# Moving the second batch's first stage, turn and low-rank step and the next pair's preparation forward in the loop of a fused Fourier and mixer kernel, and the batch's DRAM writes to the sync queue

## The chip, the cores and the metric

The kernel runs on one core of a Trainium2 chip. The metric is the device time of one execution, in microseconds (us). Executions are compared in the fast state only: a run that took over 1.5% longer than the fastest of its kernel counts as slow and is left out of the ratios. Ratios are the mean time of one kernel's fast runs over the mean of the other's fast runs of the same rounds, so they are not quite the ratios of the medians quoted beside them, which are over all runs (one slow of nine in run 3, two of six in run 7, two of 22 in run 9, one of six in run 10).

In the lines of the profile PE is TensorE, DVE is VectorE, ACT is ScalarE and POOL is GpSimd (called Pool here); SPq and ACTq are the issues of DMA transfers by the sync engine and by ScalarE. L260 is line 260 of the kernel, `teps<-g,us` means that tile teps is written from g and us, and x25 that the line stands for 25 instructions.

## The reference, cut to what matters

```python
X = np.fft.fft(np.fft.fft(x, axis=1), axis=2).real      # x: 8 batches, 3136 positions, 256 channels
h = X.transpose(0, 2, 1) @ U @ V                        # low rank (32) over the positions
u = X + h.transpose(0, 2, 1)
out = u + np.maximum(u @ w_ch1, 0.0) @ w_ch2            # 256 -> 1024 -> 256 channels
```

## The kernel before

The 8 batches go in four pairs. For each pair a loop of 13 chunks does the two channel products (`mlp1`, `mlp2`); each chunk has four steps, so a pair has 52 loop steps. Between the products, the loop also carries work for the batches to come. This other work is hung on step numbers. In the traces TensorE runs its matmuls in the order of the program, so a piece that is not ready holds up all that follows: when g was not there for the low-rank step, TensorE stood idle for 6.22 us with loop steps still to do.

The way of one batch: x is loaded, stage one (`s1`) makes z with matmuls, z is written to DRAM (`zturn`) and read back in another order as g (the **turn**), the **low-rank step** makes te from g (or, for later pairs, from z) and spreads it over the lower half of g, and stage three (`s3`) makes q, the input of the products. The **receipt** is here the time from the end of the issue of a batch's last DRAM write to the issue of its turn, where nothing else stands between the two: for the first batch 2.9 us (about 21.1 to 24.00). In pair 0 the first batch is done before the loop, but for nine of its thirteen s3 groups, which stand in steps 1 to 8. The second batch's s1, turn, low-rank step and s3 stand in the loop, as does the preparation of pair 1.

```python
def s1_single(pr, b, tiles, evacs, engines):
    ...
        evacs[n](z[:, 2 * s:2 * s + 2, :], ps[:])              # ScalarE and VectorE in turn
        if n % 2:                                              # two DRAM writes after every second step
            for i in range(2):
                engines(n)[i].dma_start(out=dst, in_=z[64 * i:64 * i + 64, ...])

def turn(pr, b, parts, engines=(nc.sync,)):                    # g <- zturn, on the sync queue
    ...
        engines[i % len(engines)].dma_start(out=g[0:64, k0:k1], in_=src[:, k0:k1, :])

def te_single(pr, b, spread):                                  # the low-rank step: 25 matmuls of 64x64 weights
    ps = psd.tile([P, 2, D], FP32, tag="ps", name="teps")
    for k in range(NK1):
        nc.tensor.matmul(ps[0:64, 0, :], us[:, k], pr.g[b][0:64, k, :], start=(k == 0), stop=(k == NK1 - 1))
    te_out(pr, b, ps, slice(0, 64), spread)                    # VectorE, then the spread on Pool

def mlp2(ch, t):
    ...
    nc.scalar.copy(om[:, 0:n], ch.po[:, 0:n, 1])               # in odd steps: ScalarE, VectorE twice,
    nc.vector.tensor_tensor(ob[:, 0:n, 0:P], ch.po[:, 0:n, 0], om[:, 0:n], op=AL.add)
    nc.vector.tensor_tensor(ob[:, 0:n, P:D], ch.po[:, 0:n, 0], om[:, 0:n], op=AL.subtract)
    ...                                                        # and four outputs on the sync queue

def place_next(nx, a, gap, s3lo):                              # the next pair
    for c, (load, fn, fd) in enumerate(load_steps(nx)):        # 8 chunks: load, fold on Pool, fold on VectorE, two s1
        for o, f in [(0, load), (4, fn), (7, fd), (9, s1[2 * c]), (10, s1[2 * c + 1])]:
            at[int(a + gap * c) + o].append(f)
    e = int(a + gap * 7) + 11
    place([lambda: (turn(nx, 0, whole), turn(nx, 1, whole))], e, e + 1)
    place(te_steps(nx, spread_pool), e, e + 3)
    place(s3_steps(nx, 0, copy_dve), s3lo, NS)
```

The PSUM tiles of s1, s3 and the low-rank step share one pool (`psd`) of two buffers.

Of the kernel before, what the change touches and what calls it, by code (L numbers as in the profile page):

```python
# [22 lines left out]
def kernel(  # L23
# [9 lines left out]
    nc = tc.nc  # L33
# [115 lines left out]
    def load_steps(pr):  # L149

        for c in range(8):
            def load(c=c):
                pr.chunks.append(load_pair_chunk(pr.p, c))
            yield load, (lambda c=c: fold_pair_chunk(pr.chunks[c])), (lambda c=c: fold_pair_chunk_d(pr.chunks[c]))
# [31 lines left out]
    def s1_single(pr, b, tiles, evacs, engines):  # L186


        if pr.z is None:
            pr.z = zpool.tile([P, 32, D], BF16, tag="z", name="z")  # L190
        z = pr.z[:, 16 * b:16 * b + 16]
        zdb = zd[pr.p % 2, b]

        def step(n, s):
            xs, l = tiles[s // 2], 4 * (s % 2)
            ps = psd.tile([P, 2, D], FP32, tag="ps", name="ps")
            todo = []
            for i in range(2):
                o = ps[64 * i:64 * i + 64]
                if s == 0 and i == 0:  # L200
                    todo.append([(o[:, 1], xs[:, 1], 0), (o[:, 0], xs[:, 0], 1), (o[:, 0], x32[b][:], 2)])
                else:
                    todo.append([(o, xs[:, l + 2 * i:l + 2 * i + 2], 0)])
            prods = []
            for parts in todo:
                pp = []
                for o, y, t in parts:
                    fe, fo, fn = (Fs[:, 3 * t + i].rearrange("p k c -> p (k c)") for i in range(3))
                    pp += [(o[..., 0:129], fe, y[..., 0:129]), (o[..., 1:128], fe, y[..., 255:128:-1]),
                           (o[..., 129:256], fo, y[..., 1:128]), (o[..., 129:256], fn, y[..., 255:128:-1])]  # L210
                prods.append(pp)
            for m in range(max(len(p) for p in prods)):
                for pp in prods:
                    if m < len(pp):
                        o, f, y = pp[m]
                        nc.tensor.matmul(o, f, y, start=(m == 0), stop=True, skip_group_check=True)  # L216
            evacs[n](z[:, 2 * s:2 * s + 2, :], ps[:])
            if n % 2:
                q = s // 2
                for i in range(2):  # L220
                    dst = bass.AP(zd.tensor, zdb.offset + (8 * q + 2 * i) * D, [[32 * D, 64], [4 * D, 2], [1, 2 * D]])
                    engines(n)[i].dma_start(out=dst, in_=z[64 * i:64 * i + 64, 4 * q:4 * q + 4].rearrange(
                        "p (i h) d -> p i (h d)", h=2))

        for n, s in enumerate([2, 3, 4, 5, 6, 7, 1, 0]):
            yield lambda n=n, s=s: step(n, s)

    def turn(pr, b, parts, engines=(nc.sync,)):
        g = gpool.tile([P, NK1, D], BF16, tag=f"g{b}", name="g")
        src = zd[pr.p % 2, b].rearrange("k cn d -> cn k d")  # L230
        for i, (k0, k1) in enumerate(parts):
            engines[i % len(engines)].dma_start(out=g[0:64, k0:k1], in_=src[:, k0:k1, :])
        pr.g[b] = g

    def te_out(pr, b, ps, hb, spread):
        te = ypool.tile([P, D], BF16, tag="te", name="te")
        nc.vector.tensor_tensor(te[64:128, :], ps[hb, 0, :], mask[hb, :], op=AL.mult)  # L237
        spread(pr.g[b], te)
# [17 lines left out]
    def te_single(pr, b, spread):  # L256
# [4 lines that stand above are left out]
        te_out(pr, b, ps, slice(0, 64), spread)  # L261

    def spread(parts):
        def run(g, te):
            src = te[64:128].bitcast(I32)
            for eng, k0, k1 in parts:
                eng.tensor_copy(g[64:128, k0:k1].bitcast(I32), src.unsqueeze(1).to_broadcast([64, k1 - k0, D // 2]))  # L267
        return run

    def two(row, a, b, n):  # L270

        v = row[:, a:a + n]
        return bass.AP(row.tensor, v.offset, [list(v.ap[0]), [b - a, 2], [1, n]])

    def s3_steps(pr, b, evac):

        if pr.q is None:
            pr.q = qpool[pr.p % 2].tile([P, 2, 6272], BF16, tag="q", name="q")

        def mm(o, k1, blk, st):  # L280
            lt = pr.g[b][:, k1, blk::2]
            r = T[:, k1, 0:64] if k1 == 0 else T[:, k1, :].rearrange("p (s j) -> p s j", s=2)
            nc.tensor.matmul(o, lt, r, start=st, stop=True, skip_group_check=True)  # L283

        def step(g, blk):
            ps = psd.tile([P, 2, 256], FP32, tag="ps", name="ps")
            k0 = 4 * g
            for u in range(4):
                us = slice(u * 64, (u + 1) * 64)
                mm(ps[:, 0, us] if k0 + u == 0 else ps[:, :, us], k0 + u, blk, u == 0)  # L290
            pl = b * 1600 + k0 * 64
            mi = 3200 + b * 1536 + (k0 - 1) * 64
            if g == 0:
                evac(pr.q[:, blk, pl:pl + 256], ps[:, 0, :])
                evac(pr.q[:, blk, mi + 64:mi + 256], ps[:, 1, 64:256])
            else:
                evac(two(pr.q[:, blk, :], pl, mi, 256), ps[:])

        def last():
            ps = psd.tile([P, 2, 2, 64], FP32, tag="ps", name="ps")  # L300
            k1 = NK1 - 1
            for blk in range(2):
                mm(ps[:, blk], k1, blk, blk == 0)
            for blk in range(2):
                evac(two(pr.q[:, blk, :], b * 1600 + k1 * 64, 3200 + b * 1536 + (k1 - 1) * 64, 64), ps[:, blk])

        for g in range(6):
            for blk in range(2):
                yield lambda g=g, blk=blk: step(g, blk)
        yield last  # L310
# [100 lines left out]
    part = [[None] * 4, [None] * 4]  # L411
# [208 lines left out]
    pairs = [first] + [Pair(p) for p in range(1, NP)]  # L620
# [3 lines left out]
    whole = [(0, NK1)]  # L624
    spread_pool = spread([(nc.gpsimd, 0, 9), (nc.gpsimd, 9, 17), (nc.gpsimd, 17, NK1)])

    def w2_fold(i):
        nc.vector.tensor_tensor(W2[:, :, i * P:(i + 1) * P], w2_f[:, :, 0], w2_f[:, :, 1],  # L628
                                op=(AL.subtract if i else AL.add))
# [39 lines left out]
    def plan(p):  # L669

        at = [[] for _ in range(NS)]

        def place(steps, lo, hi):
            steps = list(steps)
            for i, s in enumerate(steps):
                at[lo + i * (hi - lo) // len(steps)].append(s)

        def place_next(nx, a, gap, s3lo):

            s1 = list(s1_steps(nx, copy_act))  # L680
            for c, (load, fn, fd) in enumerate(load_steps(nx)):
# [7 lines that stand above are left out]
        cur = pairs[p]  # L689
        if p == 0:  # L690
            rest = []
            place(s3b0[4:8], 1, 3)
            place(s3b0[8:], 4, 9)
            place([lambda: w2_fold(0), lambda: w2_fold(1)], 2, 4)
            place([late_tables], 5, 6)
            place([load_uz], 12, 13)
            place([lambda: rest.append(pair_tables())], 6, 7)
            place([lambda: rest[0]()], 10, 11)
            place(s1_single(cur, 1, part[1], [copy_act, copy_dve] * 4, lambda n: (nc.scalar, nc.scalar)), 5, 13)
            place([lambda: turn(cur, 1, whole)], 13, 14)  # L700
            place([lambda: te_single(cur, 1, spread_pool)], 18, 19)
            place(s3_steps(cur, 1, copy_dve), 20, 32)
            place_next(pairs[1], 12, 2.5, 43)
        else:
            place(s3_steps(cur, 1, copy_dve), 3, 18)
            if p + 1 < NP:
                place_next(pairs[p + 1], 0, 3.4, 40)
        return at

    for i in range(len(chunks) + 1):  # L710
        cur = chunks[i] if i < len(chunks) else None
# [45 lines left out]
```

## Time and profile before

| | before |
|---|---|
| median | 491.05 us (489.51 to 491.84, 3 runs) |
| span of the profiled execution | 487.4 us |
| TensorE busy | 451.9 us |
| first wait: the low-rank step for g | 6.22 us, at 81.5 us |
| second wait: pair 1's s3 for g | 4.51 us, at 146.4 us |
| TensorE at half clock in the loop, up to pair 1 | 55.9 to 59.3, 86.6 to 96.8 and 151.4 to 154.8 us |

The lines themselves stand in the prediction below. The loop starts at 35.65 us with step 0. Step 2, which starts at 39.36 us, is used as a zero mark further down, as all that lies before it is the same code in all kernels here.

### The profile page before, as it was taken

How to read it: one execution, taken by the hardware profiler on the slowest of the kernel's cores; microseconds unless marked ns; L12 is line 12 of the kernel's file. 1: busy time of each engine (PE TensorE's matmuls, PEld its weight loads, DVE VectorE, ACT ScalarE, POOL GpSimd, SP SyncE). 2: the span in 40 equal slices, each digit the busy share in tenths (PEclk: the TensorE clock that was granted, in tenths of full speed). 3: DMA queues.
4: the chain of work that ended last, by engine and by line, in shares of the span. 5: the costliest groups of instructions: out<-in, count | busy, mean ns of one | idle time of the engine just before them, and what ended most of it. 6: DMA issues, size and time to landing. Idle time of an engine off the chain costs nothing.

```text
span 487.4 us, 9451 instructions
## 1 busy us (share of the span) xinstructions
PE 451.9 (93%) x3685; PEld 317.9 (65%) x3685; DVE 223.6 (46%) x512; ACT 286.1 (59%) x387; POOL 138.2 (28%) x143
## 2 busy tenths in 40 slices
PE   6878896899996999999999999999999999999992
PEld 2545564567774776766786776676777777767672
DVE  8954431086632537646425447647144344211211
ACT  6436355167752566677746556777655655666660
POOL 8442302295406025336042026534050000000000
PEclk9889899599998999999999999999999999999998
DMA  9978448568659245766386265576492222223322
GB/s 155 220 168 121 116 117 176 149 181 241 218 139 183 66 103 159 226 199 208 107 151 183 66 173 142 169 246 184 125 167 67 66 67 66 66 71 75 82 60 72
DMA packets 69297, 67.63 MB, mean 139 GB/s; under 512 B 17396, under 2 KB 62268, under 8 KB 69220
## 3 DMA queue, kind: packets, MB, share of 16 engines
q1 hardware_dynamic: 54100, 46.38, 38.3%
q0 software_dynamic: 11168, 12.92, 11.6%
q10 hardware_dynamic: 3984, 7.73, 4.7%
q8 instruction: 29, 0.48, 0.4%
q14 instruction: 16, 0.13, 0.1%
HBM read 35.95 MB, written 34.28 MB: 144 GB/s over the span
## 4 chain that ended last, share of the span: by engine, by line
PE 72%; DVE 10%; DMA 8%; SPq 3%; ACT 3%; issue 2%; ACTq 0%; POOL 0%; DVEq 0%; POOLq 0%
PE hps L334 29%; PE ops L345 28%; PE ps L283 4%; PE ops L348 4%; DMA g<-zturn 3%; DMA out_dram<-ob 3%; SPq L360 2%; PE ps L172 2%; ACT hT L336 2%; DVE q L79 2%; PE teps L260 2%; DMA xs<-in_x_dram 2%; PE teps L248 1%; DVE yb L122 1%; DVE ob L356 1%
## 5 line engine op out<-in xcount | busy, mean ns | idle before, releaser
L336 ACT ACTIVATE hT<-hps 128x1024 bf16<-128x1024 f32 (+1 forms) x208 | 202.8, 976 | 151.2 <-PE hps L334 142.0
L345 PE MATMUL ops<-W_91,hT 128*128 128x256 bf16 x1568 | 227.3, 275 | 1.1 <-DVE W_91 L628 1.1
L345 PEld LDWEIGHTS <-hT 128*128 128x128 bf16 x1568 | 146.3, 99 | 35.6 <-issue 0.8
L355 DVE TENSOR_TENSOR ob<-ops,om 128x256 f32<-128x256 f32 (+1 forms) x100 | 41.9, 419 | 195.0 <-ACT om L354 191.5
L334 PE MATMUL hps<-q,W1p 128*128 128x512 bf16 (+1 forms) x448 | 107.0, 362 | 2.4 <-DVE q L79 1.8
L334 PE MATMUL hps<-q,W1m 128*128 128x512 bf16 x384 | 100.0, 384 | 0.2 <-ACT hT L336 0.2
L131 POOL TENSOR_TENSOR y<-xa,xb 98x1020 f32<-98x1020 f32 (+1 forms) x24 | 54.8, 2282 | 126.2 <-DMA xa<-in_x_dram 123.0
L79 DVE CAST q<-ps 128x512 bf16<-128x512 f32 (+3 forms) x120 | 64.5, 559 | 32.4 <-PE ps L283 27.4
L334 PEld LDWEIGHTS <-W1p 128*128 128x128 bf16 x448 | 41.0, 98 | 30.2 <-issue 6.2
L348 PEld LDWEIGHTS <-q 128*128 128x128 bf16 x392 | 38.7, 99 | 22.6 <-issue 2.2
L334 PEld LDWEIGHTS <-W1m 128*128 128x128 bf16 x384 | 35.8, 99 | 26.4 <-issue 2.3
L283 PE MATMUL ps<-T,g 128*128 128x128 bf16 (+1 forms) x400 | 37.5, 219 | 7.2 <-DMA g<-zturn 4.5
L354 ACT COPY om<-ops 128x256 f32<-128x256 f32 (+1 forms) x100 | 36.8, 368 | 9.2 <-PE ops L345 8.3
L76 ACT CAST z<-ps 128x512 bf16<-128x512 f32 x57 | 33.5, 588 | 13.1 <-PE ps L172 10.9
L356 DVE TENSOR_TENSOR ob<-ops,om 128x256 f32<-128x256 f32 (+1 forms) x100 | 40.9, 409 | 0.0
L267 POOL COPY g<-te 64x1024 int32<-64x1024 int32 (+1 forms) x21 | 21.6, 1075 | 61.0 <-DVE te L237 61.0
L348 PE MATMUL ops<-Bp,q 128*128 128x128 f16 x200 | 38.6, 220 | 0.0
L283 PEld LDWEIGHTS <-g 128*128 128x128 bf16 x400 | 29.6, 98 | 13.1 <-POOL g L267 5.0
L348 PE MATMUL ops<-Bm,q 128*128 128x128 f16 x192 | 37.4, 221 | 0.0
L102 POOL DMA_INDIRECT xb<-in_x_dram,idx x24 | 25.4, 1059 | 10.9 <-PE ps L216 6.0
L122 DVE TENSOR_TENSOR yb<-y 98x508 bf16<-98x508 f32 (+1 forms) x24 | 27.2, 1134 | 0.8 <-POOL y L131 0.8
L172 PE MATMUL ps<-yb,F 98*128 98x258 bf16 (+1 forms) x108 | 18.9, 265 | 2.6 <-DVE q L79 2.4
(129 smaller groups left out, 220.3 us busy)
## 6 DMA issues: line engine op xcount, KB each, us to landing
out_dram<-ob SPq DMA_DIRECT2D x392, 64.0 KB
xa<-in_x_dram SPq DMA_DIRECT2D x24, 392.0 KB
g<-zturn SPq DMA_DIRECT2D x7, 800.0 KB
zturn<-z ACTq DMA_DIRECT2D x9, 512.0 KB
xs<-in_x_dram POOLq DMA_DIRECT2D x16, 196.0 KB, 8.6
w_f<-in_moe_w_ch_dram SPq DMA_DIRECT2D x2, 1024.0 KB
zturn<-z ACTq DMA_DIRECT2D x3, 448.0 KB
zturn<-z ACTq DMA_DIRECT2D x9, 128.0 KB
```

Source lines behind the costliest of these rows:

```text
L76: nc.scalar.copy(o, i)
L79: nc.vector.tensor_copy(o, i)
L122: nc.vector.tensor_tensor(o[:, :, 1:128], i[:, :, 1:128], i[:, :, 255:128:-1], op=AL.add)
L131: nc.gpsimd.tensor_tensor(ck.y[:, 0:n, 1:256], ck.xa[:, 0:n, 1:256], rb[:, :, 255:0:-1], op=AL.add)
L283: nc.tensor.matmul(o, lt, r, start=st, stop=True, skip_group_check=True)
L334: nc.tensor.matmul(ps[:, i, 0:n], (W1p if ch.sg > 0 else W1m)[:, blk, j], q[:, blk, c0:c0 + n], start=(blk == 0), stop=(blk == 1))
L336: nc.scalar.activation(ch.h[:, 2 * jp:2 * jp + 2, 0:n], ps[:, :, 0:n], AF.Relu)
L345: nc.tensor.matmul(ps, ch.h[:, j, t * P:(t + 1) * P], W2[:, j, :], start=(j == 0 and t % 2 == 0), stop=(j == JT - 1), skip_group_check=True)
L348: nc.tensor.matmul(ps[:, j], q[:, j, tk], (Bp if ch.sg > 0 else Bm)[:, j], start=False, stop=False, skip_group_check=True)
L354: nc.scalar.copy(om[:, 0:n], ch.po[:, 0:n, 1])
L355: nc.vector.tensor_tensor(ob[:, 0:n, 0:P], ch.po[:, 0:n, 0], om[:, 0:n], op=AL.add)
L356: nc.vector.tensor_tensor(ob[:, 0:n, P:D], ch.po[:, 0:n, 0], om[:, 0:n], op=AL.subtract)
```

## The change

The intent: do the second batch's stage one three steps sooner, so that its turn is back when TensorE comes to the low-rank step; keep ScalarE free of DMA issues; and start the next pair's loads four steps sooner, so that its turn too is back in time. Two things of no urgency are put off: the late tables (W1m and others) and the two loads of UZ, the table for the low-rank step of the later pairs. The whole change:

```diff
-            place([late_tables], 5, 6)
-            place([load_uz], 12, 13)
+            place([late_tables], 8, 9)
+            place([load_uz], 24, 25)
 ...
-            place(s1_single(cur, 1, part[1], [copy_act, copy_dve] * 4, lambda n: (nc.scalar, nc.scalar)), 5, 13)
-            place([lambda: turn(cur, 1, whole)], 13, 14)
-            place([lambda: te_single(cur, 1, spread_pool)], 18, 19)
-            place(s3_steps(cur, 1, copy_dve), 20, 32)
-            place_next(pairs[1], 12, 2.5, 43)
+            place(s1_single(cur, 1, part[1], [copy_act, copy_dve] * 4, lambda n: (nc.sync, nc.sync)), 2, 10)
+            place([lambda: turn(cur, 1, whole)], 10, 11)
+            place([lambda: te_single(cur, 1, spread_pool)], 15, 16)
+            place(s3_steps(cur, 1, copy_dve), 17, 29)
+            place_next(pairs[1], 8, 2.6, 44)
```

## The prediction

> **What bounds the kernel now.** I read the page first, then who waited for whom on TensorE, the timeline of TensorE and of the sync queue, the clock by the microsecond, and the chain of waits around the first loop steps.
>
> ```profile
> PE 451.9 (93%) x3685; PEld 317.9 (65%) x3685; DVE 223.6 (46%) x512; ACT 286.1 (59%) x387; POOL 138.2 (28%) x143
> PE   6878896899996999999999999999999999999992
> PEclk9889899599998999999999999999999999999998
> ```
> TensorE is the bound: 451.9 of 487.4 us busy. In the 40 slices of 12.2 us the poor ones are few: slice 8 (85 to 97 us) at clock 0.5, slice 13 (146 to 158 us) at busy 0.6.
>
> ```profile
> PE teps L260 <- DMA g<-zturn: 6.2, 1, 6.2
> PE ps L283 <- DMA g<-zturn: 4.5, 1, 4.5
> PE hps L334 <- DVE q L79: 1.8, 1, 1.8
> ```
> Columns: total us, times, longest. These three are all before 155 us; after 160 us TensorE waits 3.1 us in all. So only the start and the hand-over to pair 1 can give time.
>
> ```profile
> 29.15 2.91 PE L260 MATMUL teps<-g,us 64*64 64x256 bf16 x25
> ...
> 87.69 5.49 PE L260 MATMUL teps<-g,us 64*64 64x256 bf16 x25 [6.22 <-DMA g<-zturn]
> 93.11 1.89 PE L334 MATMUL hps<-q,W1m 128*128 128x512 bf16 x4
> ...
> 96.72 1.08 PE L334 MATMUL hps<-q,W1m 128*128 128x512 bf16 x4
> ```
> The same 25 low-rank matmuls take 2.91 us warm and 5.49 us after the wait. The step after them takes 96.72 - 93.11 = 3.61 us where a plain step takes 1.85 (73.92 to 75.77). The wait thus costs 6.22 + 2.58 + 1.76 = 10.6 us.
>
> ```profile
> 86.00:87.00 1.00, 0.00 (x0) 0.00 (x0) 0.00 (x0) 0.00 (x0) 0.00 (x0) 0.79 1.06 221
> 96.00:97.00 1.00, 1.00 (x7) 0.64 (x6) 0.00 (x0) 0.06 (x1) 0.92 (x2) 0.59 0.00 0
> ```
> The last three columns are clock, DMA share, GB/s. The clock fell near 86.5 us, 5 us into the gap, and came back near 96.7 us.
>
> ```profile
> 73.47 2.45 SPq L666 DMA_DIRECT2D UZ<-uturn  x2
> 76.03 1.46 SPq L99 DMA_DIRECT2D xa<-in_x_dram  x1
> 77.60 2.45 SPq L360 DMA_DIRECT2D out_dram<-ob  x4
> 80.09 0.65 SPq L232 DMA_DIRECT2D g<-zturn  x1
> ```
> Why the turn (the read of g from DRAM) is late: its last DRAM write was issued on the ACT queue by 72.34 us, but the sync queue first issued two UZ loads, an x load and four outputs.
>
> ```profile
> 51.01 0.69 DVE z L79
> 51.70 0.03 ACTq L222
> 51.73 0.04 issue
> 51.77 0.59 ACTq L222
> 52.36 0.04 issue
> 52.40 0.67 ACTq L222
> 53.07 0.05 issue
> 53.12 1.02 ACT hT L336
> ```
> The chain before the 1.8 us wait at 54 us: ScalarE stood at its own DMA issues, waiting for VectorE's z, before its next activation; om, ob and the q of loop step 8 then came late.
>
> [...] The 64x64 matmuls did not warm the clock in 5.49 us. [...] Here 2.9 us passed from the end of the first batch's last write issue (about 21.1) to its turn (24.00), and that is the figure I use. [...] The trace shows writes taking 0.6 us each to issue on either queue.
>
> **The change part by part.** A loop step is a quarter of a chunk. From the timeline: 0.86 us of first product + 0.99 of second = 1.85; a spectral group (s3) adds 0.22, a stage-one step (s1) 0.56, the last s1 about 0.8. Step 2 starts at 39.36, step 4 is at 42.07, step 5 at 45.43, step 9 at 59.90, step 18 at 79.46 us.
>
> *Stage one to steps 2 to 9.* Same matmuls. Two of the eight now stand beside the W2 fold, for which TensorE waits until 44.22. Their PSUM buffers come free at about 42.0 (ScalarE's q cast, 41.41 + 0.60) and 41.8. So: s1 at 42.0 to 42.56, product to 43.43, s1 to 43.99, product to 44.86, second product from 44.86 instead of 44.22. Two steps of 0.56 hidden for a delay of 0.64: gain 0.5. Data: the first x tile for it is issued to 32.58 with a median landing of 9.5 us, so it is there by about 41 to 42.
>
> *Writes from the ACT to the sync queue.* ScalarE loses eight issues of 0.6 us and, more important, its waits for VectorE. Step 5 then ends at 44.86 + 0.99 + 0.22 + 0.56 + 2.73 = 49.4, step 7 at 54.9. In step 8 the product needs the q cast of step 7: second product ends 54.05, om to 54.4, ob to 55.2, cast to 55.8. So a stall of about 0.7 us stays in place of 1.8[...]. Step 9 starts near 58.3 with seven s1 done, against 59.90 with four: ahead by 1.6 + 3 x 0.56 = 3.3 us, the gain of both parts together.
>
> *The turn.* Step 9 ends at 58.3 + 1.85 + 0.8 = 61.0. om, ob and z end at about 62.1, but the sync queue first issues four outputs (61.45 + 2.44 = 63.9), then the two writes (65.1); receipt 2.9 makes 68.0. The turn lands 7.5 us after its issue (80.09 to 87.69 before; 4.65 of it is 819 kB at 176 GB/s as in the 84 to 86 us range, so I let the absence of UZ save nothing). That gives 75.5. TensorE is ready after steps 10 to 14 and step 15's products: 61.0 + 6 x 1.85 = 72.1. A wait of about 3.2 us (75.5 - 72.1, less a little) remains of 6.22: gain 3.0, and 4.3 more (2.58 + 1.76) if the clock stays up, to which I give one in four: 3.0 + 1.1 = 4.1.
>
> *Next pair's loads from step 8, its turn at step 37 instead of 40, its s3 at 44 instead of 43.* Before, three steps lay between turn and use and TensorE waited 4.51 us, with the clock halved to 154.8: step 43 takes from 151.33 to 155.07 less its s3, 3.5 against 1.85, so 1.7. Cost 6.2. Now counted from the end of step 36: z cast and write issue 1.9, receipt 2.9, two turns 7.2 (143.63 to 150.8): landed at 12.0. TensorE: three short steps with their low-rank parts, 3 x 2.63 = 7.9, step 40 1.85, steps 41 to 43 bound by the 1.02 us activation, 3.1, step 44 1.85: 14.7. The wait is gone with 2.7 us of margin; the idle edges of steps 41 to 43 cost 3 x 0.16 = 0.5. Gain 5.7.
>
> *Late tables and UZ at steps 8 and 24.* W1m is wanted from step 12, UZ from step 37: nothing on the path, and UZ's 2.45 us leave the turn's way (counted there).
>
> Sum: 3.3 + 4.1 + 5.7 = 13.1 us.
>
> **The rivals.** (1) The turn comes in time: if landing takes 6 us as for the first batch (24.00 to 30.65, idle queues) and the writes 2 us, the wait is under 1 us and the clock stays up: 6 us better than mine, 471. For it: less traffic ahead of the turn. Against: its in-order place behind four outputs. (2) The sync queue becomes the new bound: 392 outputs at 0.6 us, plus 4.8 us of writes in steps 3 to 9, and it stands still until the last write is confirmed, so outputs and the next x loads slip. Four ob buffers and 3.6 us of issue in a 5.4 us pair of steps speak against it; if it bites, the turn slips 3 us more: 482 to 485. (3) The earlier stage-one stalls for its x tiles or PSUM pairs (two buffers shared with s3, VectorE busy with the 2.36 us fold): 1 to 3 us back, 479 to 481. (4) The second wait was hidden anyway: no, TensorE's own row shows it idle.
>
> **Range and chances.** 491.05 - 13.1 = 478. The two big terms are each all or nothing by the clock, about 4 and 2 us, and the stage-one part may be off by 2: 471 to 485. Faster by over 2% means under 481.2: 0.77; within 2%: 0.21; slower: 0.02, as no part adds work to TensorE.
>
> **What would show it.** The wait of the low-rank step for g at 2 to 4 us near 72 us, not 6.2; the turn issued near 68 us, held by the write's landing rather than by UZ; no wait of s3 for g near 140 us; the q wait of step 8 under 1 us; no half clock at 56 us and none at 151. A new wait of s1 on xs or PSUM near 42 us, x folds waiting into TensorE's path, or a turn issued after 71 us would make me wrong.

## The result, and the profile after

The changed kernel takes 477.08 us in the median (475.19 to 477.19, 4 runs) against 491.44 us of the kernel before in the same rounds (4 runs): ratio 0.9707, 95% interval 0.9675 to 0.9739. It is faster by 2.9%, or 14.4 us. The span of the profiled execution is 475.3 us, 12.1 us less. All these runs are fast ones.

The page of the changed kernel, parts 1 and 2:

```profile
PE 447.6 (94%) x3685; PEld 316.8 (67%) x3685; DVE 223.5 (47%) x512; ACT 287.1 (60%) x387; POOL 138.6 (29%) x143
PE   7769997899999999999999999999999999999992
PEclk9998997999999999999999999999999999999997
```

TensorE has 4.3 us less busy time for the same 3685 matmuls, because fewer of them ran at half clock: in the loop 55.9 to 59.3, 86.6 to 96.8 and 151.4 to 154.8 us before, and 77.9 to 84.7 us after. The slices with clock 0.5 and with busy share 0.6 in mid-loop are gone.

Who waited for whom on TensorE (total us, times, longest):

```profile
PE ps L172 <- DVE q L79: 4.0, 5, 1.5
PE teps L260 <- DMA g<-zturn: 3.5, 3, 2.8
...
PE hps L334 <- DVE q L79: 0.7, 1, 0.7
```

The low-rank step still waits for g, but 2.8 us in place of 6.2. (The other 0.7 us of that line belong to the first batch, ahead of the loop.) The wait of s3 for g has left the list. The q wait of step 8 is 0.74 us, and the clock stays at 1.00 after it (52 to 66 us). On top stands a wait that has grown: the later pairs' s1 waits 4.0 us in all for VectorE's q casts, against 2.4 before, and once, in pair 1's first s1, for 1.5 us, where the longest was 0.8.

TensorE around the low-rank step (start, duration, operation, and in brackets the idle time before it):

```profile
76.08 3.78 PE L260 MATMUL teps<-g,us 64*64 64x256 bf16 x25 [2.83 <-DMA g<-zturn]
79.79 1.89 PE L334 MATMUL hps<-q,W1m 128*128 128x512 bf16 x4
...
83.39 1.70 PE L334 MATMUL hps<-q,W1m 128*128 128x512 bf16 x4
...
85.91 0.56 PE L283 MATMUL ps<-T,g 128*128 128x64 bf16 x8
87.97 0.40 PE L172 MATMUL ps<-yb,F 98*128 98x258 bf16 x2 [1.50 <-DVE q L79]
```

The clock by the microsecond (third column from the right):

```profile
77.00:78.00 1.00, 1.00 (x11) 0.97 (x10) 0.00 (x0) 0.00 (x0) 0.00 (x0) 0.95 0.92 294
78.00:79.00 1.00, 1.00 (x6) 0.82 (x5) 0.00 (x0) 0.00 (x0) 0.00 (x0) 0.50 0.83 276
...
84.00:85.00 1.00, 1.00 (x5) 0.36 (x3) 0.00 (x0) 0.00 (x0) 1.00 (x2) 0.63 0.60 197
```

So the clock did fall, though the wait was 2.83 us and not 6.22, and it fell inside the low-rank step: about two thirds of the 25 matmuls (up to 77.9 us) are fast, the rest slow, and so is all up to about 84.7 us.

How the turn came to its place, from the chain of waits (start, duration, what):

```profile
65.94 0.28 SPq L222
66.22 0.04 issue
66.27 2.47 DMA zturn<-z
68.74 0.02 SPq L232
68.76 0.03 issue
68.79 7.25 DMA g<-zturn
```

The sync queue stands at the turn until the last write has landed, issues it at 68.79, and 7.25 us later g is there.

The new 1.5 us wait, in VectorE's timeline:

```profile
86.56 0.42 DVE L355 TENSOR_TENSOR ob<-ops,om 128x256 f32<-128x256 f32 x1 [2.96 <-ACT hT L336]
86.90 0.41 DVE L356 TENSOR_TENSOR ob<-ops,om 128x256 f32<-128x256 f32 x1
87.23 1.27 DVE L79 CAST q<-ps 128x256 bf16<-128x256 f32 x4
```

Step 17 carries two s3 groups, which take both PSUM buffers, and the first s1 of pair 1, which needs one of them back. Step 17 is an odd step, so om and ob go ahead of the casts. Before, the first s3 stood in step 20, an even one, and s1 in step 21.

**Where the time came from.** From step 2 to the first product of pair 1 it takes 170.13 - 39.36 = 130.8 us before and 158.25 - 40.29 = 118.0 us after: 12.8 us gained. Nothing is gained outside this stretch: the part before step 2 is 0.9 us longer in this execution (the same code starts step 2 anywhere from 38.76 to 43.02 us in the profiles of this study), and from pair 1's first product to the end the two spans have 317.3 and 317.0 us.

### The profile page after: what moved, and what is told of

It is laid out like the page before. It is cut to its first block, busy times and chain, and to the rows that moved or that the text cites. A ratio compares the mean times of both kernels' runs of the same rounds, so it can differ in the third digit from the quotient of the medians.

```text
span 475.3 us, 9454 instructions
## 1 busy us (share of the span) xinstructions
PE 447.6 (94%) x3685; PEld 316.8 (67%) x3685; DVE 223.5 (47%) x512; ACT 287.1 (60%) x387; POOL 138.6 (29%) x143
## 4 chain that ended last, share of the span: by engine, by line
PE 79%; DMA 8%; DVE 5%; ACT 3%; issue 2%; SPq 1%; POOL 0%; DVEq 0%; POOLq 0%; ACTq 0%
PE hps L334 32%; PE ops L345 32%; PE ops L348 4%; DMA xs<-in_x_dram 4%; PE ps L283 3%; DMA g<-zturn 3%; PE ps L172 2%; ACT hT L336 2%; PE teps L248 2%; PE ps L216 2%; DVE q L79 2%; DMA zturn<-z 1%; DVE ob L355 1%; PE teps L260 1%; ACT om L354 1%
## 5 line engine op out<-in xcount | busy, mean ns | idle before, releaser
L345 PE MATMUL ops<-W,hT 128*128 128x256 bf16 x1568 | 225.4, 273 | 0.0
L79 DVE CAST q<-ps 128x512 bf16<-128x512 f32 (+3 forms) x120 | 64.5, 559 | 28.9 <-PE ps L283 24.4
L354 ACT COPY om<-ops 128x256 f32<-128x256 f32 (+1 forms) x100 | 36.8, 368 | 8.0 <-PE ops L345 7.6
L122 DVE TENSOR_TENSOR yb<-y 98x508 bf16<-98x508 f32 (+1 forms) x24 | 29.1, 1213 | 0.0
```

Of the source, the lines that this page charges most:

```text
L79: nc.vector.tensor_copy(o, i)
L122: nc.vector.tensor_tensor(o[:, :, 1:128], i[:, :, 1:128], i[:, :, 255:128:-1], op=AL.add)
L345: nc.tensor.matmul(ps, ch.h[:, j, t * P:(t + 1) * P], W2[:, j, :], start=(j == 0 and t % 2 == 0), stop=(j == JT - 1), skip_group_check=True)
```

## The experiments

Theory: three independent gains, as predicted (stage one with its queue, the first wait, the second wait). Rivals are named with each run. All runs gave correct results. "Gain" below is (1 - ratio) x 491.4 us. Each run was timed in five rounds.

### 1. The next pair's schedule alone, on the kernel before

```diff
-            place_next(pairs[1], 12, 2.5, 43)
+            place_next(pairs[1], 8, 2.6, 44)
```

> The kernel before with one part of the change alone: the next pair's loads from step 8, its turn at step 37, its s3 from step 44. Theory of the three parts (sum of independent waits): the 4.5 us wait of s3 for g at the hand-over and the 1.7 us of half clock after it go, 0.5 us comes back in the activation-bound steps 41 to 43: 5.7 us less, ratio 0.988; no wait of s3 for g after 130 us, the 6.2 us wait of the low-rank step stays within 2 us. Rival (the second wait was hidden, or only follows from the first): ratio 0.998 to 1.002.

Measured: 485.51 us, ratio 0.9894 (0.9847 to 0.9942), gain 5.2 us. In its trace the low-rank step waits 6.9 us, and s3's wait for g at the hand-over is gone. The rival, a second wait that only follows from the first, falls.

### 2. All but the next pair's schedule

```diff
-            place_next(pairs[1], 8, 2.6, 44)          # of the changed kernel
+            place_next(pairs[1], 12, 2.5, 43)
```

> The changed kernel with the next pair's schedule put back (loads from step 12, turn at step 40, s3 from 43). Theory of the three parts: stage one, writes, turn and low-rank step keep their gain, the hand-over wait of 4.5 us returns with its half clock: 5.7 us slower than the changed kernel, ratio to before about 0.982. Rival (the first wait causes the second): the hand-over wait stays away, ratio 0.971.

Measured: 484.11 us, ratio 0.984 (0.9792 to 0.9887), gain 7.9 us. The second wait is back, at 4.75 us. The gains of runs 1 and 2 add to 13.1 us; the whole change has 14.4 us. The two halves add up within the intervals.

### 3. The queue of the writes alone, on the kernel before

```diff
-    ... [copy_act, copy_dve] * 4, lambda n: (nc.scalar, nc.scalar)), 5, 13)
+    ... [copy_act, copy_dve] * 4, lambda n: (nc.sync, nc.sync)), 5, 13)
```

> The kernel before with only the second batch's DRAM writes on the sync queue. Theory of the three parts: the q wait of step 8 falls from 1.8 to about 0.7 us and no half clock follows it (2.8 us less), but the writes now stand behind outputs in the turn's queue and the turn is up to 1.2 us later (about 1 us more): ratio 0.994 to 0.998. Rival (most of the gain is ScalarE freed of its issues and waits): ratio 0.985 or lower.

Measured: 486.33 us, ratio 0.9897 (0.9863 to 0.9932), gain 5.1 us: a miss, more than the theory expected and less than the rival's 0.985 or lower. The q wait of step 8 fell to 0.74 us with no half clock after it (1.00 from 52 to 84 us), as expected; the 2.8 us named there are 1.1 us of wait and, as an estimate, 1.7 us for the 3.4 us at half clock before (55.9 to 59.3). What was wrong is the turn: it is issued at 76.92 us, that is 36.8 us after step 2, against 40.7 before; 3.9 us sooner and not 1.2 us later. The sync queue of this run, around the turn:

```profile
66.09 2.41 SPq L360 DMA_DIRECT2D out_dram<-ob  x4
68.61 2.58 SPq L666 DMA_DIRECT2D UZ<-uturn  x2
71.30 2.36 SPq L222 DMA_DIRECT2D zturn<-z  x2
...
76.92 0.63 SPq L232 DMA_DIRECT2D g<-zturn  x1
```

Before, the same four outputs began at 70.12 us (30.8 us after step 2), here at 66.09 (26.0). Of these 4.8 us, 2.9 are a lead that TensorE has by step 12 (65.31 - 40.10 = 25.2 us after step 2, before 67.45 - 39.36 = 28.1), through the shorter q wait and the kept clock. The other 1.9 fit ScalarE, which makes om, for which the outputs wait, and no longer stands at DMA issues. Work that I had counted as standing in the turn's way was itself late, in part for the reason that the change removes.

### 4. The low-rank step two steps later

```diff
-            place([lambda: te_single(cur, 1, spread_pool)], 15, 16)   # of the changed kernel
-            place(s3_steps(cur, 1, copy_dve), 17, 29)
+            place([lambda: te_single(cur, 1, spread_pool)], 17, 18)
+            place(s3_steps(cur, 1, copy_dve), 19, 31)
```

> The changed kernel with the second batch's low-rank step at step 17 and its s3 from step 19 to 31, two steps later, so that 3.7 us more of product work lies between turn and use. Theory: the 2.8 us wait that is left goes, the low-rank matmuls take 2.9 in place of 3.8 us, the half clock after it (2.4 us) goes: 6 us less than the changed kernel, ratio to before about 0.959. Rival (the time just moves on to the spread by the Pool engine and to s3): wait of s3 for g near step 19, ratio stays at 0.969 to 0.972.

Measured: 478.09 us, ratio 0.974 (0.9699 to 0.9782): no gain over the changed kernel. The lines of TensorE and of Pool:

```profile
77.08 3.52 PE L260 MATMUL teps<-g,us 64*64 64x256 bf16 x25 [1.30 <-DMA g<-zturn]
```
```profile
86.91 3.10 POOL L267 COPY g<-te 64x1152 int32<-64x1152 int32 x3 [4.86 <-DMA xb<-in_x_dram,idx]
```

The wait fell to 1.3 us, not to zero, as the turn took 9.2 us to land. The clock fell all the same after it, from about 79.2 to 86.0 us. And te was ready at 81.05 us, but Pool began the spread only at 86.91: a gather of x, issued at 81.08, stands ahead of it in Pool's order now, and the trace puts the 4.86 us down to that gather's landing. The rival holds: the 1.5 us won at the low-rank step went again, 0.6 us in a wait of s3 for Pool's g and 1.0 us in longer waits of pair 1's s1 for q (0.73, 1.54 and 0.26 us, against one of 1.50).

### 5. The idle time filled

```diff
-            place([lambda: te_single(cur, 1, spread_pool)], 15, 16)   # of the changed kernel
+            place([lambda: keep_warm(12), lambda: te_single(cur, 1, spread_pool)], 15, 16)
```

`keep_warm(12)` is twelve 128x512 matmuls whose result is not used.

> The changed kernel with twelve 128x512 matmuls of no use (2.6 us) put between the products of step 15 and the low-rank step, where TensorE waits 2.8 us for g. It takes the idle time away and leaves the wait for g. Theory (the wait halves the clock): the low-rank matmuls take 2.9 in place of 3.8 us and the half clock after them goes: 3 us less, ratio to before 0.965. Rival (the 64x64 matmuls[...] let the clock fall by themselves): half clock in or after the low-rank step as in the changed kernel, ratio 0.969 to 0.972.

Measured: 474.79 us, ratio 0.9695 (0.9645 to 0.9745).

```profile
75.35 2.91 PE L260 MATMUL teps<-g,us 64*64 64x256 bf16 x25
```
```profile
76.00:78.00 2.00, 2.00 (x21) 1.95 (x19) 0.00 (x0) 0.00 (x0) 0.00 (x0) 1.00 0.88 269
```

The trace decides for the theory: the low-rank step takes 2.91 us and the clock stays at 1.00 throughout. Of the 3 us in hand here, 1.46 us went to a wait of s3 for Pool's spread, which TensorE now reached first. In the times the gain over the changed kernel is not told from noise, as the intervals overlap.

### 6. The last two writes on the ACT queue

```diff
-    lambda n: (nc.sync, nc.sync)), 2, 10)             # of the changed kernel
+    lambda n: (nc.scalar, nc.scalar) if n == 7 else (nc.sync, nc.sync)), 2, 10)
```

> The changed kernel with the last two of the eight DRAM writes on the ACT queue again, the other six on the sync queue. They no longer stand behind four outputs (2.4 us). Theory (in-order place on the sync queue sets the turn): the turn is issued 2.5 us sooner, the wait for g falls from 2.8 to 0.3 to 0.5 us: 2.5 us less, ratio 0.966, and 0.960 if the clock then stays up. Rival (DMA traffic sets when the turn lands): it lands at most 1 us sooner, ratio 0.969 to 0.972.

Measured: 475.12 us, ratio 0.9689 (0.9648 to 0.9731), not told from the changed kernel. The turn and its reader:

```profile
66.52 0.62 SPq L232 DMA_DIRECT2D g<-zturn  x1
```
```profile
75.42 4.95 PE L260 MATMUL teps<-g,us 64*64 64x256 bf16 x25 [3.23 <-DMA g<-zturn]
```

Counted from step 2 (39.10 us here), the writes' issue ended at 24.4 us against 26.6 in the changed kernel, so the 2.2 us were won. Then the receipt took 3.0 us (63.51 to 66.52) against 1.9 (66.88 to 68.79), and the turn 8.9 us against 7.3. It landed at 36.3 us against 35.8. The theory that the place on the sync queue alone sets the landing falls for this step: in this one profile a longer receipt and a longer flight took back all that the queue gave. What made them longer is not shown.

### 7. All writes back on the ACT queue

```diff
-    lambda n: (nc.sync, nc.sync)), 2, 10)             # of the changed kernel
+    lambda n: (nc.scalar, nc.scalar)), 2, 10)
```

> The changed kernel with all eight DRAM writes back on the ACT queue. Theory: ScalarE waits for VectorE's z again, the q wait of step 8 is back at 1.8 us with half clock after it (2.8 us) and the outputs before the turn come later (the queue change alone on the kernel before gave 3 us in the profile); the writes gain up to 2.5 us by not standing behind outputs. 1 to 3 us more than the changed kernel: ratio 0.973 to 0.977. Rival (the queue does not matter once the steps are moved): 0.971 or lower, q wait of step 8 under 1 us.

Measured: 481.02 us, ratio 0.9767 (0.9712 to 0.9821). The queue is worth 0.9767 - 0.9707 = 0.006 here, or 2.9 us, as expected; the intervals overlap a little. It rests on the sorting of the runs: two of the six (486.03 and 486.18 us) count as slow, and with them the ratio would be about 0.981. Its profiled execution was a slow one, so nothing is read from its trace.

### 8. The low-rank step in three pieces

```diff
-            place([lambda: te_single(cur, 1, spread_pool)], 15, 16)   # of the changed kernel
-            place(s3_steps(cur, 1, copy_dve), 17, 29)
+            place(te_pieces(cur, 1, spread_pool), 17, 20)             # the same 25 matmuls as 9 + 8 + 8
+            place(s3_steps(cur, 1, copy_dve), 20, 32)
```

> The changed kernel with the low-rank step in three pieces of 9, 8 and 8 matmuls after the products of steps 17, 18 and 19, and the second batch's s3 from step 20 to 32. Theory[...]: between full-array products the clock stays at 1 and no wait for g is left: 5 to 6 us saved there, 1 to 2 us given back in waits of the pair's s1 for PSUM, as s3 now meets more of it: ratio 0.960 to 0.964. Rival (VectorE's evacuations set this stretch): ratio 0.970 to 0.975, waits of s1 and s3 on VectorE's q of 6 us or more.

Measured: 481.18 us, ratio 0.9812 (0.977 to 0.9854): slower than the changed kernel, and a miss for both. The clock did stay at 1.00 through the three pieces (76.4 to 83.9 us) and g was waited for no longer, but:

```profile
PE ps L298 <- POOL g L282: 8.1, 1, 8.1
```
```profile
92.93 3.10 POOL L282 COPY g<-te 64x1152 int32<-64x1152 int32 x3 [5.87 <-DMA xb<-in_x_dram,idx]
```

(Line numbers are shifted by the added function.) The last piece ended at 83.9 us, and the spread began at 92.93 us, again right when the gather ahead of it had landed (86.09 + 6.68 = 92.77). In this wait the clock fell too, from 91.1 to 97.9 us. With run 4 this is the second sight of it. Whether this is a wait of the program or of the engine is left open; that the copy stood, for 4.9 and 5.9 us, is measured.

### 9. The UZ loads alone, on the kernel before

```diff
-            place([load_uz], 12, 13)
+            place([load_uz], 24, 25)
```

> The kernel before with only the UZ loads moved from step 12 to step 24. Theory (the turn waits for its place on the sync queue): the turn is issued 2.5 us sooner, near 77.6 us, the wait for g falls from 6.2 to about 3.7 us, the clock still halves: ratio 0.995. Rival (the landing is set by DMA traffic or by the write receipt, not by the queue's order): wait for g 5.5 us or more, ratio 0.998 to 1.002.

Measured: 489.04 us, ratio 0.9941 (0.9919 to 0.9964), gain 2.9 us. The turn is issued at 74.70 us and the low-rank step starts at 82.12: the wait is 2.9 us, and the flight of 7.4 us is about what it was with UZ ahead (7.6). So UZ costs its place in the queue, as predicted; that it costs no bandwidth fits this one pair of profiles, though flights differ by 2.4 us over the study. Counted from step 2 (38.76 us) the turn is 4.8 us sooner, more than the 2.45 us of the two issues. Some of it is the clock: step 8 waits 1.8 us for q as before, but in this profile the clock stays at 1.00 after it (54 to 64 us), where before it fell to 0.50 (55.9 to 59.3). Part of the gain goes again later: the hand-over wait of this run is 6.3 us against 4.5.

### 10. The moved steps alone

```diff
-    lambda n: (nc.sync, nc.sync)), 2, 10)             # of the changed kernel
+    lambda n: (nc.scalar, nc.scalar)), 2, 10)
-            place_next(pairs[1], 8, 2.6, 44)
+            place_next(pairs[1], 12, 2.5, 43)
```

> The moved steps of the second batch with its tables, but the writes on the ACT queue and the next pair's schedule as before. Theory (parts add up): the changed kernel's 0.971, plus 0.006 for the queue, plus 0.0115 for the hand-over: ratio 0.985 to 0.991, the hand-over wait of 4 to 5 us and the q wait of step 8 at 1.6 us or more both back. Rival (the queue move was only worth something with the old steps): 0.980 to 0.983.

Measured: 484.6 us, ratio 0.985 (0.9809 to 0.9891), at the edge of what was expected. Both waits named there are back (5.3 and 1.6 us). The low-rank step waits 1.37 us and then runs in 2.89 us, as at full clock (2.91 for the first batch before the loop), where in run 4 a wait of 1.30 us was followed by half clock. The queue's worth beside run 2 is only 0.001; the three estimates (5.1 us in run 3, 2.9 in run 7, 0.5 here) agree only within intervals of about 2 to 4 us, and its size is not settled better than that. Beside run 9 (0.9941), which has UZ moved as well, the moved steps and late tables are worth 0.009, or 4.5 us, and the intervals do not meet. The tables were not moved alone.

**Which waits half clock followed.** The wait of the low-rank step for g in each profile, and the time that its 25 matmuls then took:

| profile | wait for g | 25 low-rank matmuls |
|---|---|---|
| first batch before the loop (before) | none | 2.91 us |
| filled (runs 5 and 11) | none | 2.91 |
| filled in part (run 12) | 0.52 us | 2.89 |
| run 4 | 1.30 | 3.52 |
| run 10 | 1.37 | 2.89 |
| run 2 | 1.74 | 3.09 |
| changed kernel | 2.83 | 3.78 |
| run 9 | 2.92 | 5.43 |
| run 6 | 3.23 | 4.95 |
| run 3 | 4.95 | 5.49 |
| before | 6.22 | 5.49 |
| run 1 | 6.94 | 5.49 |

The long waits go with slow matmuls, but the order is not strict: 1.30 us was followed by half clock from about 79.2 to 86.0 us (run 4), 1.74 us by half clock from about 80.2 to 83.7 us, nearly all of it after the matmuls (run 2), and 1.37 us by none (run 10, where the products after it take 1.04 and 1.03 us). The q wait of step 8 shows the same: 1.82 us was followed by half clock before, 1.82 us in run 9 and 1.63 us in run 10 were not. So the length of the wait alone does not tell whether the clock falls. What else does is not shown; no run was made to test it.

### 11. and 12. Filled, with a faster spread, and with later loads

Run 11 joins runs 5 and 6 and gives the first 9 of the 25 te copies to VectorE. Run 12 has six filling matmuls only and puts the third and fourth x loads of pair 1 at step 16.

```diff
-    place([lambda: te_single(cur, 1, spread_pool)], 15, 16)           # of run 6
+    place([lambda: keep_warm(12), lambda: te_single(cur, 1, spread([(nc.vector, 0, 9), (nc.gpsimd, 9, 17),
+           (nc.gpsimd, 17, NK1)]))], 15, 16)                          # run 12: keep_warm(6)
-                for o, f in [(0, load), (4, fn), ...
+                for o, f in [(16 - int(a + gap * c) if nx.p == 1 and c in (2, 3) else 0, load), (4, fn), ...   # run 12
```

> The changed kernel with the twelve idle-time matmuls, the last two DRAM writes on the ACT queue, and the first nine of the 25 te copies on VectorE instead of Pool. Theory (after the wait and the clock, the Pool engine's spread is the next bound of this stretch): the wait of s3 for Pool's g (1.5 us with the idle-time matmuls alone) goes, s1's waits for q shrink by about 0.5 us: ratio 0.964 to 0.967. Rival (VectorE is as full there): ratio as with the idle-time matmuls alone, 0.969.

Measured: 475.42 us, ratio 0.967 (0.9625 to 0.9715). The ratio lies at the end of what was expected and its interval holds the rival's 0.969 too. The wait of s3 for Pool is gone from the trace, while the 1.5 us wait of s1 for q in step 17 stays.

> As the run before, with only six idle-time matmuls and the next pair's third and fourth x loads both at step 16 instead of 13 and 15, so that no gather of x is in flight with the turn. Theory (the gather takes the DMA engines from the turn): the turn lands 6.8 us after its issue in place of 7.3 to 9, the low-rank step starts about 1.5 us sooner: ratio 0.961 to 0.964. Rival (the turn's time is its own): landing stays at 7.3 us or more, ratio 0.965 or higher, and late folds show as waits of s1 for yb.

Measured: 473.83 us, ratio 0.9648 (0.9615 to 0.9682). It is the fastest kernel of the study by its median. Its interval still meets that of the changed kernel (0.9675 to 0.9739) at the edge, so "faster than the changed kernel" is likely and not shown. The turn's flight, 68.47 to 75.54, is 7.1 us with no gather in it, and the low-rank step waits 0.5 us after its six fillers:

```profile
75.54 2.89 PE L260 MATMUL teps<-g,us 64*64 64x256 bf16 x25 [0.52 <-DMA g<-zturn]
```

The ratio lies between the theory's 0.964 and the rival's 0.965, and the flight between their 6.8 and 7.3 us, so whether gathers of x slow the turn is not settled. In fast profiles where TensorE waited for g, flights without a gather beside them are 6.8 (run 2), 7.1 (run 12), 7.35 (run 1) and 8.0 us (run 10); with a gather that moved at least 11% of the engines' time they are 7.3 (the changed kernel), 8.9 (run 6) and 9.2 us (run 4). Three profiles with a gather of under 2% lie between: 7.4 (runs 3 and 9) and 7.6 us (before). The groups lean apart and overlap.

## Why the prediction was right

The predicted time is 478.0 us and the measured one 477.08. The times below are counted from the start of step 2, which came 0.93 us later in the changed kernel's profile than in that of before.

| step of the prediction | predicted | measured |
|---|---|---|
| start of step 9, with seven s1 done | 58.3 us | 59.24 - 0.93 = 58.3 |
| q wait of step 8 | 0.7 | 0.74 |
| turn issued | 68.0 | 68.79 - 0.93 = 67.9 |
| g lands | 75.5 | 76.08 - 0.93 = 75.2 |
| TensorE ready for the low-rank step | 72.1 | 73.25 - 0.93 = 72.3 |
| wait left | 3.2 | 2.83 |
| gain at the hand-over | 5.7 | 5.7 (below); 5.2 in run 1 |
| sum | 13.1 | 12.8 in the traces, 14.4 in the medians |

**The hand-over.** TensorE at the first s3 group of pair 1 and at the first product of pair 1, before and then after:

```profile
150.94 0.55 PE L283 MATMUL ps<-T,g 128*128 128x64 bf16 x8 [4.51 <-DMA g<-zturn]
170.13 1.03 PE L334 MATMUL hps<-q,W1p 128*128 128x512 bf16 x4
```
```profile
142.44 0.56 PE L283 MATMUL ps<-T,g 128*128 128x64 bf16 x8
158.25 1.03 PE L334 MATMUL hps<-q,W1p 128*128 128x512 bf16 x4
```

From step 40's product to the first product of pair 1 it took 170.13 - 138.34 = 31.8 us before and 158.25 - 135.69 = 22.6 after. Before, this stretch also held the three low-rank pieces (1.20 + 1.20 + 1.09 = 3.5 us), which the change moved ahead of it. What is left, 28.3 - 22.6, is 5.7 us. The turn was issued 5.7 us after the end of step 36 and not 4.8, and s3 stood 13.9 us after it and not 14.7, so the margin was thinner than the 2.7 us predicted; it held. (Most of the second is that a short step with its low-rank piece takes 2.41 us, 128.58 to 130.99, and not 2.63.)

**The first wait.** Its mechanism was right, and so was the size of what was left and the reason for it: four outputs, two writes, a receipt, a flight. That the turn was issued on time is partly luck: the issue of the writes ended 0.85 us later than predicted (66.88 - 0.93 = 65.95 against 65.1), and the receipt took 1.9 us and not 2.9. The gain of this part was sized less well. The prediction put 4.1 us on it, 3.0 for the wait and 1.1 for one chance in four that the clock stays up. The clock did neither: it fell late, half-way into the low-rank step, which then took 3.78 us and not 5.49, and it came back only 1.3 us into step 17 (83.39 to about 84.7). And the 1.5 us wait of s1 in step 17 was not in the prediction at all. It looked at the wait for g and took s3's new place for neutral; that an odd step puts om and ob ahead of the casts was in its own argument about step 8 and was not applied here.

**The sum, part by part.** The low-rank step stands three product steps sooner after the change, 3 x 1.85 = 5.55 us. Up to TensorE being ready for it the gain is (81.47 - 39.36) - (73.25 - 40.29 + 5.55) = 3.6 us, against 3.3 predicted. From there to step 40, with the low-rank pieces of 3.5 us taken off, it is (138.34 - 81.47) - (135.69 - 73.25 - 5.55 - 3.5) = 3.5 us, against 4.1. The hand-over gives 5.7 as predicted. That makes the 12.8; the two misses nearly cancel.

**Slips without harm.** The 176 GB/s beside the 819 kB is not that of 84 to 86 us, which show 184 and 193, but that of 148 to 149 us. And the landing of the first batch's turn, called 6 us in rival 1, is 6.65 by the numbers given there (24.00 to 30.65).

**The rivals.** A turn in time (rival 1) did not happen. A sync queue as bound (rival 2) did not happen: run 3 shows outputs sooner, not later. A stall of stage one for its x tiles (rival 3) came to 0.78 us, at step 2, but no later than the PSUM wait that the prediction had counted there: s1 started at 42.67 - 0.93 = 41.7 us, against 42.0 predicted. That the second wait was hidden (rival 4) is refuted by run 1.

**What stayed open.** How the gain divides. Tried singly, the next pair (run 1, 5.2 us), the queue (run 3, 5.1), UZ (run 9, 2.9) and the steps with the tables (run 10 beside run 9, 4.5) add to 17.7 us, more than the 14.4 of the whole. So some of them seem to win the same time (single gains have intervals of 1 to 3 us either way): the queue gave 5.1 us with the old steps and 0.5 to 2.9 with the new ones. The queue and UZ together with the old steps, which would show what the moved steps add to them, were not run. Also open: how much of the 7.9 us of run 2 belongs to the queue; what lengthens the flight of the turn from 6.8 to 9.2 us; and why Pool's spread stood until a gather had landed (4.86 us in run 4, 5.87 in run 8).

## What to carry to other kernels

When TensorE works in program order, read each of its waits back to the issue of the transfer, and count what stands ahead of that issue in its queue: here two loads of no urgency and an engine that waited for another engine's result before it issued a write. Count the half clock that follows a wait as part of it, but don't expect to win it back by shortening the wait: half clock followed 1.30 us in run 4, and it did not follow 1.82 us in run 9. With the gap filled (run 5), or the small matmuls set between the products (run 8), the clock was 1.00 throughout the low-rank step. When a step is moved later, look at what then stands ahead of its followers on every engine: twice here the spread of a later low-rank step stood on Pool behind a gather, and TensorE then waited for it 0.6 us (run 4) and 8.1 us (run 8).
